# Batch 0's channel-128 transform ahead of the cosine transform, its row copied by ScalarE, the second weight chunk's products on GpSimd

## The chip, the cores and the metric

One NeuronCore of one Trainium2 chip runs the whole program. The metric is the device time of one execution in microseconds (us). One profiled execution per kernel gives a trace; the others are only timed. Engines are named as in the profile: PE is TensorE (PEld its weight loads), DVE is VectorE, ACT is ScalarE, POOL is GpSimd, and SPq is the queue of SyncE, which issues most DMAs.

## The reference, cut to what matters

```python
# x: (8, 3008, 256) float32; w_in: (256, 2048), w_out: (2048, 256), both float64
X = np.fft.fft(np.fft.fft(x, axis=1), axis=2).real     # FNet mixing
h = X.reshape(8 * 3008, 256) @ w_in
g = np.where(h > 0, h, np.exp(np.minimum(h, 0)) - 1)   # ELU
return g @ w_out
```

## The kernel before: the parts that the change touches

The kernel computes the sequence transform as matrix products with cosine and sine matrices (`MC`), using the symmetries of both axes: the input is folded to even and odd parts, and each batch has a cosine result `Rr` and a sine result `Ir` for channels 0 to 127. Channel 128 has no partner and is a single row. The channel transform is folded into the first weight matrix: `Wc` and `Ws` are made from `w_in` by small products ("folds"), chunk by chunk of 256 columns. The main loop then has 376 steps; each makes a cosine product `H <- Rr, Wc`, an even part `E` on VectorE, which adds channel 128 (`Rb` times a per-column factor `wex`), and a sine product `H <- Ir, Ws`, followed by ELU and the second layer. Row 127 of `Ir` carries the channel-128 row too.

The weights arrive as 64-bit floats and are turned into 32-bit ones by bit operations, in chunks. Each chunk has four parts; a "shared" one has its arithmetic on ScalarE and GpSimd:

```python
def fields(self):            # VectorE: exponent to a scratch t ("u", "v", ..., one buffer each), mantissa to dst
    ...
def power(self):             # ScalarE: exponent field; if shared also lo and dst to float
    act(self.t, self.t, func=AF.Relu, scale=8.0, bias=ebias)
    if self.shared: ...
def round(self):             # shared: GpSimd add; else VectorE
    ...
def scale(self):             # VectorE: sign into t; shared: GpSimd multiplies dst by t; else VectorE
    ...
```

Each fold's row for channel 128 must become a column. It goes through DRAM:

```python
def put_chunk(c):            # ScalarE copies the fold from PSUM to Ws and Wc
    ...
def spread_last_row(q):      # row 127 of Ws -> wx in DRAM -> two columns of wex
    queue.dma_start(out=wx_dr[:, c], in_=Ws[127:128, c])
    queue.dma_start(out=wex[:, 2*q : 2*q + 2], in_=wx_dr[:, c].rearrange("o (f p) -> p (o f)", p=128))
```

What is emitted when is a sorted list of events `at(t, fn)`, with `T` = 4.8 for a step. Negative times are the start; the hardware engines each run their own instructions in that order.

```python
for _ in range(62):                                     # filler matmuls on zeros
    mm(idle, zero, zero[:, 0:1].to_broadcast([128, 512]), True)
...
at(-13.0, lambda: dft_now(R_even, 1, "pA")); at(-12.9, lambda: dft_now(R_even, 0, "pB"))
at(-12.8, begin_x_even)                                 # channel 128, two transforms, after the cosine ones
...
at(-5.7, lambda: nc.sync.dma_start(out=Ir[127:128, 0:RUN], in_=Rb[127:128, 0:RUN]))
at_chunk(-5.0, w1_chunks[2])
```

## Time and profile before

| | before |
|---|---|
| executions known when the prediction was made | 1994.29, 1993.30, 1985.84; profiled one 1984.7 |
| span of the trace | 1982.9 |
| TensorE busy | 1960.3 (99%) |
| first sine product / second step's even part / ninth step's even part, start | 37.84 / 46.76 / 102.19 |

In the order of time, a line has its start, its length, engine, source line, operation, what it writes and reads, the shapes and the count of instructions merged into it. In brackets stands how long the engine was idle before it and what ended that. The granted clock is the share of full speed that TensorE's clock had; half clock is 0.50. A DMA lands when its semaphore reports its data. The prediction below shows and reads the lines of the kernel before.

The second step's even part (counting from one; the steps of the source count from zero) and the ninth's serve as marks in what follows: up to the first lie the parts that the change moves, and between the two the remaining weights are converted.

### The profile page before, as it was taken

The numbers are of one execution on the slowest core, as the hardware profiler recorded it, in microseconds if no ns is written. First come the engines' busy times: TensorE is split into PE (matmuls) and PEld (weight loads), VectorE is DVE, ScalarE is ACT, GpSimd is POOL, SyncE is SP. The second block draws the span as 40 slices with busy tenths as digits, with TensorE's granted clock in tenths as the row PEclk, the third lists the DMA queues.
The fourth block names the chain that finished last, engine by engine and source line by source line (L and its number), as shares of the span: only waits on it lengthen the run. The fifth ranks groups of instructions, "written<-read, shape, count | busy, mean of one in ns | idle before, by whom it ended". The sixth has DMA issues, their size and how long they took to land.

```text
span 1982.9 us, 26811 instructions
## 1 busy us (share of the span) xinstructions
PE 1960.3 (99%) x8896; PEld 1661.3 (84%) x8896; DVE 1280.8 (65%) x2342; ACT 861.0 (43%) x1651; POOL 1333.5 (67%) x1820
## 2 busy tenths in 40 slices
PE   8899999999999999999999999999999999999998
PEld 5788888888888888888888888888888888888887
DVE  7866656666666656676566666666556765666665
ACT  3544444443444444444444443444444444344443
POOL 2678757786577756777667775678657776455655
PEclk9999999999999999999999999999999999999999
DMA  8227200121011110011100211003010110100101
GB/s 322 86 20 64 46 16 16 38 59 21 16 19 45 45 29 12 18 43 46 28 11 20 61 28 27 11 19 86 9 21 12 20 22 14 16 12 12 22 10 23
DMA packets 256044, 71.61 MB, mean 36 GB/s; under 512 B 244303, under 2 KB 245092, under 8 KB 255394
## 3 DMA queue, kind: packets, MB, share of 16 engines
q1 hardware_dynamic: 251330, 57.05, 14.5%
q0 software_dynamic: 2400, 12.59, 1.9%
q8 instruction: 70, 1.15, 0.2%
q14 instruction: 68, 0.56, 0.1%
q10 hardware_dynamic: 2176, 0.26, 0.1%
HBM read 45.02 MB, written 24.80 MB: 35 GB/s over the span
## 4 chain that ended last, share of the span: by engine, by line
PE 94%; DVE 3%; DMA 1%; ACT 1%; issue 0%; POOL 0%; DVEq 0%; POOLq 0%; ACTq 0%; SPq 0%
PE H L353 38%; PE pB L353 16%; PE pD L353 16%; PE pC L353 16%; PE pA L353 8%; DVE E L715 0%; DMA Ir<-Rb 0%; DMA xl<-in_x_dram,ix 0%; DVE o L426 0%; DVE G L741 0%; DMA wex<-wx 0%; DVE e L426 0%; DMA wx<-Ws 0%; DVE v L359 0%; ACT w L365 0%
## 5 line engine op out<-in xcount | busy, mean ns | idle before, releaser
L362 POOL TENSOR_TENSOR G<-G 128x256 f32<-128x256 f32 x1472 | 1057.5, 728 | 580.4 <-DVE G L741 466.0
L715 DVE SCALAR_TENSOR_TENSOR E<-Rb,wex,H 128x256 f32<-128x256 f32 x752 | 328.0, 478 | 608.2 <-PE H L353 603.5
L365 ACT ACTIVATE G<-H 128x512 f32<-128x512 f32 x376 | 224.5, 597 | 950.2 <-DVE G L725 950.2
L353 PE MATMUL H<-Ir,Ws 128*128 128x256 f32 x1504 | 388.6, 381 | 11.3 <-DVE E L715 6.6
L353 PE MATMUL H<-Rr,Wc 128*128 128x256 f32 x1504 | 386.4, 379 | 0.0
L353 PE MATMUL pC<-G,WT 128*128 128x256 f32 x1472 | 377.8, 379 | 0.0
L353 PEld LDWEIGHTS H<-Rr,Wc 128*128 128x128 f32 x1504 | 285.1, 190 | 53.2 <-issue 2.5
L353 PEld LDWEIGHTS H<-Ir,Ws 128*128 128x128 f32 x1504 | 277.1, 189 | 62.5 <-DVE E L715 11.6
L353 PEld LDWEIGHTS pC<-G,WT 128*128 128x128 f32 x1472 | 279.7, 190 | 38.0
L725 DVE SCALAR_TENSOR_TENSOR G<-E,H 128x512 f32<-128x512 f32 x376 | 257.4, 685 | 40.5 <-PE H L353 2.7
L741 DVE SCALAR_TENSOR_TENSOR G<-G,H 128x512 f32<-128x512 f32 x376 | 256.0, 681 | 32.2 <-ACT G L365 32.1
L741 DVE SCALAR_TENSOR_TENSOR G<-M,G 128x512 f32<-128x512 f32 x376 | 257.1, 684 | 0.0
L353 PE MATMUL pA<-G,w 128*128 128x256 f32 x800 | 234.1, 379 | 0.5 <-issue 0.5
L353 PE MATMUL pB<-G,w 128*128 128x256 f32 x800 | 234.0, 379 | 0.0
L365 ACT ACTIVATE G<-G 128x512 f32<-128x512 f32 x376 | 233.3, 620 | 0.0
L365 ACT ACTIVATE M<-G 128x512 f32<-128x512 f32 x376 | 224.2, 596 | 0.0
L365 ACT ACTIVATE M<-M 128x512 f32<-128x512 f32 x376 | 221.0, 588 | 0.1
L353 PE MATMUL pD<-G,WT 128*128 128x256 f32 x736 | 219.1, 379 | 1.5 <-DVE v L359 1.5
L353 PE MATMUL pB<-G,WT 128*128 128x256 f32 x736 | 219.2, 379 | 0.5 <-POOL G L362 0.5
L353 PE MATMUL pD<-G,w 128*128 128x256 f32 x736 | 218.9, 379 | 0.0
L353 PEld LDWEIGHTS pA<-G,w 128*128 128x128 f32 x800 | 151.9, 190 | 21.5 <-POOL w L362 0.9
L353 PEld LDWEIGHTS pB<-G,w 128*128 128x128 f32 x800 | 152.0, 190 | 20.7
(136 smaller groups left out, 1332.8 us busy)
## 6 DMA issues: line engine op xcount, KB each, us to landing
out_dram<-ot SPq DMA_DIRECT2D x496, 32.0 KB
xl<-in_x_dram SPq DMA_DIRECT2D x16, 768.0 KB
MC<-dft_mats SPq DMA_DIRECT2D x4, 1131.0 KB
out_dram<-ot SPq DMA_DIRECT2D x256, 2.0 KB
Rb<-r SPq DMA_DIRECT2D x10, 376.0 KB
raw<-in_moe_w_in_dram SPq DMA_DIRECT2D x6, 512.0 KB
raw<-in_moe_w_out_dram SPq DMA_DIRECT2D x6, 512.0 KB
out_dram<-ot SPq DMA_DIRECT2D x64, 28.0 KB
```

Of the source, the lines that this page charges most:

```text
L353: nc.tensor.matmul(out_, lhsT=lhsT, rhs=rhs, start=start, stop=stop, skip_group_check=True)
L362: pin(nc.gpsimd.tensor_tensor(out=o, in0=a, in1=b, op=op))
L365: pin(nc.scalar.activation(out=o, in_=i, func=func, **kw))
L715: nc.vector.scalar_tensor_tensor(out=S.E[:, c], in0=Rb[:, cols(i)], scalar=wex[:, f : f + 1], in1=S.H[:, c], op0=ALU.mult, op1=ALU.add,)
L725: nc.vector.scalar_tensor_tensor(out=two(S.G[:, 0:512])[:, :, ::-1], in0=two(S.E), scalar=2.0, in1=two(S.H), op0=ALU.mult, op1=ALU.subtract,)
L741: nc.vector.scalar_tensor_tensor(out=o, in0=e, scalar=-1.0, in1=h, op0=ALU.add, op1=ALU.max)
```

## The change

It takes away the one DMA that TensorE waits for, brings channel 128 to the front so that its row is there early, drops 16 fillers, and gives chunk 1's products to GpSimd. Chunk 1's fold moves behind the first sine product, and chunk 2 is no longer converted ahead of the first even part but after it, beside chunk 3. The core of the diff (cut):

```diff
-            c in (2, 3),
+            c in (1, 2, 3),                       # chunks with shared arithmetic
...
-        e = spool.tile([128, GW], FP, tag="G", bufs=3, name="xb")       # 128 x 768, the value broadcast
...
+        e = spool.tile([128, 6], FP, tag="xe0", bufs=1, name="xe0")     # broadcast as TensorE reads it
...
-    for _ in range(62):
+    for _ in range(46):
...
+    at(-13.1, lambda: dft_now(state["x_even"], 1, "pC"))     # ahead of R_even's transforms
+    at(-13.1, lambda: dft_now(state["x_even"], 0, "pD"))
...
-    at(-5.7, lambda: nc.sync.dma_start(out=Ir[127:128, 0:RUN], in_=Rb[127:128, 0:RUN]))
-    at_chunk(-5.0, w1_chunks[2])
...
+    at(-10.88, lambda: act(Ir[96:128, 0:RUN], Rb[96:128, 0:RUN]))
...
+    at(0.95, w1_chunks[2].fields)                 # after the first even part, beside chunk 3
+    at(0.96, w1_chunks[2].power)
+    at(0.97, w1_chunks[2].round)
+    at(1.7, w1_chunks[2].scale)
...
-        t = (c - 2) * T + 4.7 if c > 1 else 1.0   # fold of chunk 1: behind the first sine product
+        t = (c - 2) * T + 4.7 if c > 1 else 2.3
```

More of the change, by code (lines that the diff above doesn't have):

```diff
@@ L480, in fold_first @@
         vtt(d, a, g, ALU.subtract)
-        e = spool.tile([128, GW], FP, tag="G", bufs=3, name="xb")
-        vtt(
-            e[:, 0:768].rearrange("p (m d) -> p m d", d=128),
-            a.unsqueeze(2).to_broadcast([128, 6, 128]),
-            g.unsqueeze(2).to_broadcast([128, 6, 128]),
-            ALU.add,
-        )
+        e = spool.tile([128, 6], FP, tag="xe0", bufs=1, name="xe0")
+        vtt(e, a, g, ALU.add)
         return e
@@ L497, in dft_mms @@
                 ps[:, 0:n],
-                stat[:, m * width : m * width + 128],
+                stat[:, m * width : m * width + 128]
+                if width > 1
+                else stat[:, m : m + 1].to_broadcast([128, 128]),
                 MC[ri, kodd][:, c : c + n],
@@ L528, in mms @@
         def mms(self, par, ps):
-            dft_mms(ps, self.ri, self.kodd, par, self.stat, 127 if self.ri else 128)
+            width = 1 if self.first else 127 if self.ri else 128
+            dft_mms(ps, self.ri, self.kodd, par, self.stat, width)
             if par:
@@ L1041, with begin_x_even @@
     at(-25.8, w1_chunks[0].round)
+    def begin_x_even():
+        state["x_even"] = Dft(0, 0, 0, fold_first(L_first), ring=Rb, first=True)
     at(-25.5, load_rest)
@@ L1044 @@
     at(-24.9, w1_chunks[0].scale)
-    at(-24.8, lambda: fold_now("c2 e2 E2 o3 o2 c0 e0 c1 e1 E0 EO0"))
+    at(-24.8, lambda: fold_now("c2 e2 E2 o3 o2"))
+    at(-24.5, begin_x_even)
+    at(-24.4, lambda: fold_now("c0 e0 c1 e1 E0 EO0"))
     at(-20.8, w2_chunks[2].load)
@@ L1052 @@
     at(-12.9, lambda: dft_now(R_even, 0, "pB"))
-    def begin_x_even():
-        xb = fold_first(L_first)
-        state["x_even"] = Dft(0, 0, 0, xb, ring=Rb, first=True)
-        dft_now(state["x_even"], 1, "pC")
-        dft_now(state["x_even"], 0, "pD")
-    at(-12.8, begin_x_even)
+    at(-13.1, lambda: dft_now(state["x_even"], 1, "pC"))
+    at(-13.1, lambda: dft_now(state["x_even"], 0, "pD"))
     at(-13.05, lambda: spread_last_row(0))
+    at(-11.5, lambda: state["x_even"].copy())
     at(-11.0, lambda: fold_now("O2 o0 o1 O0 EO2"))
-    at_chunk(-10.0, w1_chunks[1])
-    at(-8.5, R_even.copy)
-    at(-8.4, R_even.plus)
-    at(-8.3, R_even.minus)
-    at(-8.2, lambda: dft_now(I_even, 1, "pA"))
-    at(-8.1, lambda: dft_now(I_even, 0, "M"))
-    at(-6.0, lambda: state["x_even"].copy())
-    at(-5.9, lambda: state["x_even"].plus())
-    at(-5.8, lambda: state["x_even"].minus())
-    at(-5.7, lambda: nc.sync.dma_start(out=Ir[127:128, 0:RUN], in_=Rb[127:128, 0:RUN]))
-    at_chunk(-5.0, w1_chunks[2])
+    at(-10.9, lambda: state["x_even"].plus())
+    at(-10.89, lambda: state["x_even"].minus())
+    at(-10.88, lambda: act(Ir[96:128, 0:RUN], Rb[96:128, 0:RUN]))
+    at(-10.8, w1_chunks[1].fields)
+    at(-10.79, R_even.copy)
+    at(-10.78, w1_chunks[1].power)
+    at(-10.6, R_even.plus)
+    at(-10.59, R_even.minus)
+    at(-10.5, lambda: dft_now(I_even, 1, "pC"))
+    at(-10.5, lambda: dft_now(I_even, 0, "M"))
+    at(-10.4, w1_chunks[1].round)
+    at(-10.3, w1_chunks[1].scale)
+    at(0.95, w1_chunks[2].fields)
+    at(0.96, w1_chunks[2].power)
+    at(0.97, w1_chunks[2].round)
+    at(1.7, w1_chunks[2].scale)
     at(1.3, lambda: fold_now("EO1"))
@@ L1103 @@
     for c in range(1, 8):
-        t = (c - 2) * T + 4.7 if c > 1 else 1.0
+        t = (c - 2) * T + 4.7 if c > 1 else 2.3
         at(t, lambda c=c: fold_chunk(c))
-        t = (c - 1) * T + 1.4 if c > 1 else 2.0
+        t = (c - 1) * T + 1.4 if c > 1 else 3.0
         at(t, lambda c=c: put_chunk(c))
```

## The prediction

> **What bounds the kernel now.** I read the busy shares first, then the chain that ended last by engine, then the table of stretches to find where TensorE is idle, then TensorE's order of time and the other engines' around that place.
>
> Page of the kernel before, parts 1 and 4:
>
> ```profile
> PE 1960.3 (99%) x8896; PEld 1661.3 (84%) x8896; DVE 1280.8 (65%) x2342; ACT 861.0 (43%) x1651; POOL 1333.5 (67%) x1820
> ...
> PE 94%; DVE 3%; DMA 1%; ACT 1%; issue 0%; POOL 0%; DVEq 0%; POOLq 0%; ACTq 0%; SPq 0%
> ```
>
> TensorE is the bound. Only 1982.9 - 1960.3 = 22.6 us of the span are without a matmul, and no change that leaves the matmuls alone can win more. The stretches (us, busy time and count of each engine, granted clock, DMA share, GB/s) say where they lie:
>
> ```profile
> 0.00:20.00 20.00, 18.86 (x74) 8.91 (x75) 13.45 (x28) 3.38 (x7) 2.97 (x13) 1.00 0.93 362
> 20.00:30.00 10.00, 10.00 (x33) 6.01 (x32) 9.41 (x18) 2.63 (x5) 1.17 (x2) 1.00 1.05 392
> 30.00:34.00 4.00, 3.17 (x14) 2.27 (x12) 3.24 (x8) 1.33 (x4) 2.56 (x2) 1.00 0.99 406
> 34.00:38.00 4.00, 0.16 (x1) 0.19 (x2) 3.23 (x4) 3.50 (x7) 2.35 (x2) 0.91 1.00 389
> 38.00:41.00 3.00, 3.00 (x7) 2.19 (x8) 1.07 (x2) 0.79 (x3) 1.61 (x2) 0.56 1.06 377
> 41.00:48.00 7.00, 6.03 (x23) 4.09 (x22) 4.43 (x9) 1.82 (x4) 1.85 (x1) 1.00 0.21 69
> 48.00:100.00 52.00, 46.21 (x201) 37.13 (x200) 45.27 (x77) 28.58 (x57) 31.22 (x43) 1.00 0.25 82
> ```
>
> The diff touches the first 50 us only. There are 1.14 us idle at the start, 4.67 in 33 to 38, 0.97 before 48, and 5.8 in 48 to 100, where VectorE is 87% busy converting weights. DMA is full (share about 1) until about 42 us. TensorE in order of time at that place:
>
> ```profile
> 1.14 16.29 PE L353 MATMUL M<-zero 128*128 128x512 bf16 x62 [1.14 <-DVE zero L340]
> ...
> 37.84 2.04 PE L353 MATMUL H<-Ir,Ws 128*128 128x256 f32 x4 [4.67 <-DMA Ir<-Rb]
> 39.68 2.55 PE L353 MATMUL pA<-MC,e 128*128 128x376 f32 x6
> 42.07 2.06 PE L353 MATMUL pB<-MC,e 128*128 128x376 f32 x6
> 43.97 1.89 PE L353 MATMUL H<-w,CC 128*128 128x256 f32 x8
> 45.69 1.03 PE L353 MATMUL H<-Rr,Wc 128*128 128x256 f32 x4
> ```
>
> 62 filler matmuls on zeros end at 17.3. The first sine product then waits 4.67 us for a 3 KB row, Ir<-Rb, sent at 28.50 into a full DMA queue and landed at 37.71 (the trace's semaphore record): 9.2 us. At half clock its four matmuls take 2.04 instead of 1.03 and the next six 2.55 instead of 2.07, 1.5 us more. The even part of step 1 starts at 46.76 when TensorE has made its product.
>
> **What the Trainium skill says.** "TensorE: Matmul & The Clock Gate", Part 1 (What's actually happening): the clock falls to half after an idle window of about 3.4 us, on a free-running 3413 ns grid. The trace agrees: half clock for 3.413 us from 37.248, after idleness from 33.2. "DMA: Bandwidth & Descriptors", Queues, rings and completion order: each DMA engine consumes its ring in order; the row's 9.2 us behind matrices and weights agree. "SBUF — State Buffer", Who interferes with whom: GpSimd and a two-port VectorE operation exclude each other; one tensor_scalar of the conversion took 1.51 us beside GpSimd against 0.42 elsewhere, so it agrees. "ScalarE: Activation LUTs", What ACT_TABLE_LOAD costs: an ACTIVATE is 186 ns + 0.833 ns an element; the trace's 512-element ones take 0.60 to 0.66, so my estimate from that page for the new 752-element row copy is 0.81.
>
> **The change part by part.**
> - Fillers 62 to 46. Warm ones start 0.217 apart, so the first fold starts 16 x 0.217 = 3.5 earlier, at 13.8. The cosine matrix lands at 15.48, when this fold ends. Unpaid by itself: fillers are no work.
> - Channel 128 first, its stationary operand one column broadcast instead of a 128x768 tile: takes one VectorE add of 0.95 away for one of 0.16. The six transforms (about 1.9 each) run 15.6 to 27.0 instead of 19.0 to 30.4. VectorE's last odd fold ends at 23.85 - 0.8 = 23.1, just when TensorE wants it. I assume a broadcast weight load costs the same 0.19.
> - The row DMA becomes a ScalarE copy on 32 partitions, 0.81, after the Rb sum and before the Ir sums overwrite rows 96 to 126. The DMA wait goes. Rr is then complete at about 26.4, Ir at 28.6.
> - First step: its wex column comes 11.4 us after ScalarE's put of chunk 0 (19.86 to 31.28 in the trace); that put now ends at 16.4, so wex is there at 27.8. Even part 28.6 to 29.4, sine product 29.5 to 30.4, against 37.84: **8 us earlier here**.
> - Chunk 1's two products go to GpSimd (1.29 and 1.27). VectorE loses two instructions of 0.69, ScalarE gains two (0.66 and 0.61). Chunk 1 is ready at 29.9, its fold runs 30.4 to 32.1 (now behind the sine product).
>
> **What takes the gain back.** The next matmuls are R_odd on the odd cosine matrix, which landed at 34.72 in the trace. That DMA is issued at 20.33 in a queue that runs full, with nothing changed in front of it. So TensorE idles about 32.1 to 34.8 and R_odd starts about 4.9 earlier than 39.68, not 8. The idle time is below 3.4, so I expect no half clock.
>
> A second brake lies in step 1, whose even part needs wex for chunk 1: put by ScalarE, row out to DRAM, column back in. Before:
>
> ```profile
> 37.80 0.36 ACT L365 ACTIVATE Ws<-H 128x256 f32<-128x256 f32 x1
> ...
> 38.19 0.31 SPq L392 DMA_DIRECT2D wx<-Ws  x1
> ...
> 41.50 0.37 SPq L394 DMA_DIRECT2D wex<-wx  x1
> ```
>
> The column landed at 44.43, a slack of 2.3 to 46.76. In the new order two weight chunks (2 and 3) are converted together after the first even part, and the next one (second matrix, chunk 0) needs the scratch u that chunk 2's second GpSimd product still reads. Worked out: fields of chunk 2 at 29.4 to 30.1, ScalarE's three operations for it 29.9 to 31.8, for chunk 3 31.8 to 33.6; GpSimd's products 31.8 to 33.1, 33.7 to 35.0, 35.0 to 36.3, 36.3 to 37.5. So the fields of the next chunk are free at 36.3, and through the port lock end at about 38.2 (before: 37.23). ScalarE's three operations end at 39.8, and Ws is put at 40.1, **two us later than before**. The DMA backlog still ends near 42.4. Row and column took 6.2 together in the backlog, about 3.4 without; I take 4.5, so wex lands at about 44.6.
>
> Meanwhile R_odd ends at 38.6, the fold at 40.3, step 1's cosine product at 41.3: they wait for wex. Step 1's even part starts at 44.6 instead of 46.76. From there all engines keep the old order (I compared it engine by engine: it is the same), so the rest shifts by **2.1 us**. Sum: 8 gained at the first step, 3 lost to the matrix, 3 more to the scratch and the wex round trip.
>
> **Rivals.**
> 1. The full gain: 4.67 idle + 1.5 half clock + the earlier start, 5 to 8 us. For it: the wait is real and on the chain. Against: the landing at 34.72. It would give about 1986.
> 2. Only the matrix binds: 4.9 us, 1988.4. For it: wex for chunk 1 could come sooner if the conversion overlaps better than I worked out. Against: the scratch u exists once.
> 3. Nothing or a small loss: the wex trip behind the backlog takes 6.2 again (46.3), TensorE's idle 41 to 45 fills a window and costs half clock, so 0 to +1.5. For it: VectorE bound in 48 to 100 us. Against: the backlog ends soon after the row is sent.
> 4. Spread between executions: three runs from 1985.84 to 1994.29 and a profiled one at 1984.7, larger than any of these.
>
> **Range and chances.** 1993.3 - 2.1 = 1991.2 from the median; the mean of the four executions is 1989.5, less 2.1 is 1987.4. As I can't tell which group the new runs fall into, I say 1990. The range, 1983 to 1995.5, covers the four executions (1984.7 to 1994.3) shifted by -2 to +1. Two per cent is 40 us, more than the 22.6 us of all idle TensorE time; slower by 40 us would need damage in the steady state, whose order is unchanged. So within 2% is nearly sure: 0.98, 0.01 to each side.
>
> **What the profile after will show.** No Ir<-Rb DMA and no wait on it; first sine product near 29.5 (my sum of the front is wrong if it is beyond 31); TensorE's largest early wait before pA<-MC,e, on the MC DMA, near 34.8, then one before the second H<-Ir,Ws near 45, released by VectorE's E after the wex DMA. Ws put for chunk 1 near 40, not 38. 46 fillers, VectorE some 2 us less busy, GpSimd some 2.6 more. Wrong would be: R_odd well before 34; the put before 38 (then the gain is 4 to 5); a slower broadcast weight load; or idle TensorE time after 100 us that was not there.

## The result

Six executions of the changed kernel took 1984.04 to 1986.31, median 1984.97; six of the kernel before have the median 1986.23. The ratio is 0.9982 with a 95% interval from 0.9963 to 1.0001, which takes in 1. Such a ratio is the mean time of one kernel's fast runs over that of the other's of the same rounds, so not quite the ratio of the medians. "Fast" there means not over 1.5% above the fastest; executions that are 4 to 12 us longer than the rest (0.2% to 0.6%) pass as fast. There are such executions, and they matter here. I call those over 1990 us long and the others quick; the cut is mine. The quick ones before: 1985.84, 1986.42, 1986.04, 1985.47, mean 1985.94. The changed kernel's six, all quick: mean 1985.05. So the change is worth 0.9 us in that comparison, where the prediction had about 2 from its working and 3.3 (1993.3 less 1990) from its base.

The page of the changed kernel, parts 1 and 4, shows TensorE as busy as before; its 2.3 us less are 4.2 less of fillers (12.09 against 16.29) and some half clock more. Sixteen fillers of 0.217 would be 3.5; the other 0.7 is luck, as nine fillers instead of twelve ran at about half speed at the start (0.427 apart):

```profile
PE 1958.0 (99%) x8880; PEld 1661.6 (84%) x8880; DVE 1281.2 (65%) x2340; ACT 862.8 (44%) x1654; POOL 1336.2 (67%) x1822
...
PE 94%; DVE 2%; DMA 2%; ACT 1%; issue 0%; POOL 0%; DVEq 0%; POOLq 0%; ACTq 0%; SPq 0%
```

The stretches of the changed kernel (us; busy time and count of PE, PEld, DVE, ACT, POOL; granted clock; DMA share; GB/s):

```profile
34.00:38.00 4.00, 4.00 (x15) 2.50 (x14) 1.58 (x2) 0.19 (x1) 4.00 (x4) 1.00 1.01 388
38.00:41.00 3.00, 1.32 (x7) 0.81 (x5) 3.00 (x5) 2.21 (x5) 0.80 (x2) 1.00 0.96 346
41.00:48.00 7.00, 3.08 (x9) 2.27 (x10) 6.10 (x11) 3.82 (x8) 2.63 (x2) 0.62 0.27 83
48.00:100.00 52.00, 47.08 (x199) 38.69 (x198) 44.01 (x74) 26.93 (x55) 30.92 (x43) 0.95 0.25 82
```

The hole of 34 to 38 us is gone. A new one has come at 38 to 48: TensorE is busy 4.4 of 10 us there. The granted clock falls to 0.62 in 41 to 48 and is 0.95 over the next 52 us, where it had been 1.00. TensorE in order of time:

```profile
29.98 1.10 PE L353 MATMUL H<-Ir,Ws 128*128 128x256 f32 x4 [1.45 <-DVE E L713]
30.92 1.89 PE L353 MATMUL H<-w,CC 128*128 128x256 f32 x8
33.56 2.13 PE L353 MATMUL pA<-MC,e 128*128 128x376 f32 x6 [0.75 <-DMA MC<-dft_mats]
...
41.18 1.13 PE L353 MATMUL H<-Rr,Wc 128*128 128x256 f32 x4 [1.86 <-ACT Wc L365]
46.05 2.07 PE L353 MATMUL H<-Ir,Ws 128*128 128x256 f32 x4 [3.74 <-DVE E L713]
47.92 2.82 PE L353 MATMUL pA<-MC,o 128*128 128x376 f32 x6
```

The first sine product starts at 29.98 instead of 37.84, 7.9 us earlier. The second one starts at 46.05 instead of 47.68, only 1.6 earlier: TensorE waited 1.86 for ScalarE's put of chunk 1 and 3.74 for the even part, and took 2.07 and 2.82 at half clock where 1.13 and 2.06 are full-clock lengths. The even part was held by its column:

```profile
40.50 0.36 ACT L365 ACTIVATE Ws<-H 128x256 f32<-128x256 f32 x1
...
40.88 0.31 SPq L392 DMA_DIRECT2D wx<-Ws  x1
...
42.07 0.36 SPq L394 DMA_DIRECT2D wex<-wx  x1
...
45.13 0.87 DVE L713 SCALAR_TENSOR_TENSOR E<-Rb,wex,H 128x256 f32<-128x256 f32 x2 [0.86 <-DMA wex<-wx]
```

Why the put came at 40.50 and not near 38 is in GpSimd's and VectorE's order of time:

```profile
35.98 2.49 POOL L362 TENSOR_TENSOR w<-w,pow 128x512 f32<-128x512 f32 x2
...
37.28 1.48 DVE L214 TENSOR_SCALAR pow<-w 128x512 int32<-128x512 int32 x1 [2.42 <-DMA raw<-in_moe_w_in_dram]
```

VectorE could not start the next chunk's fields before GpSimd's product for chunk 2, the first of the two that begin at 35.98, had read the scratch u. (The profile names a DMA as the releaser; that DMA was long in, and the start at 37.28 is the end of one product of about 1.25.) It then took 1.48 beside the second product, against 0.41 for the next one.

How the start of the even part moved against the kernel before, step by step, in the profiled executions (counted from one):

| even part of step | 1 | 2 | 3 | 4 | 5 | 6 | 7 | 9 | 100th |
|---|---|---|---|---|---|---|---|---|---|
| before, us | 31.97 | 46.76 | 56.65 | 65.75 | 75.23 | 83.46 | 89.89 | 102.19 | |
| changed, difference | -3.00 | -1.63 | -1.39 | -1.37 | -0.55 | -0.66 | -0.22 | -0.21 | -0.25 |

So 1.6 us are won at the second even part, and 1.4 of them are gone by the seventh. What is left at the ninth stays to the start of the last step. After that it goes too: TensorE waits 0.33 for GpSimd before some of its last products (at 1973.08), and the two traces end at 1982.9 (before) and 1983.1 (changed).

How far such marks can be trusted shows in b_late, an experiment below: up to 100 us it is the kernel before, yet its second even part lies at +0.47 and its ninth at +0.70. And the trace of the kernel before is one of its quickest executions (1984.7, where its quick means are 1985.9 to 1986.7), so differences against it understate a gain. Differences below about 0.7 between single traces decide nothing by themselves.

Three terms make up that 1.4. The interval from the second to the third even part is 10.13 instead of 9.89: half clock from 42.6 to 49.4. The one from the fourth to the fifth is 10.29 instead of 9.48: the column of the fifth step took 7.2 us from its put to its landing, instead of 6.4, beside the loads of batch 1. Its even part, before and then changed:

```profile
75.23 0.87 DVE L715 SCALAR_TENSOR_TENSOR E<-Rb,wex,H 128x256 f32<-128x256 f32 x2 [0.32 <-DMA wex<-wx]
```

```profile
74.67 0.87 DVE L713 SCALAR_TENSOR_TENSOR E<-Rb,wex,H 128x256 f32<-128x256 f32 x2 [1.13 <-DMA wex<-wx]
```

The interval from the sixth to the seventh is 6.88 instead of 6.43: TensorE, which had waited 3.01 in the fifth step, ran at half clock from 76.75 to 80.16 and was still behind. The lines of that place, before and then changed:

```profile
76.15 1.13 PE L353 MATMUL H<-Ir,Ws 128*128 128x256 f32 x4 [2.20 <-DVE E L715]
77.12 1.89 PE L353 MATMUL pB<-G,w 128*128 128x256 f32 x8
```

```profile
75.60 1.13 PE L353 MATMUL H<-Ir,Ws 128*128 128x256 f32 x4 [3.01 <-DVE E L713]
76.57 3.43 PE L353 MATMUL pB<-G,w 128*128 128x256 f32 x8
```

The same eight products take 3.43 instead of 1.89.

### The profile page after: what moved, and what is told of

It reads as the page before. It is cut to its first block, busy times and chain, and to the rows that moved or that the text cites. A ratio compares the mean times of both kernels' runs of the same rounds, so it can differ in the third digit from the quotient of the medians.

```text
span 1983.1 us, 26783 instructions
## 1 busy us (share of the span) xinstructions
PE 1958.0 (99%) x8880; PEld 1661.6 (84%) x8880; DVE 1281.2 (65%) x2340; ACT 862.8 (44%) x1654; POOL 1336.2 (67%) x1822
## 3 DMA queue, kind: packets, MB, share of 16 engines
HBM read 45.02 MB, written 24.80 MB: 35 GB/s over the span
## 4 chain that ended last, share of the span: by engine, by line
PE 94%; DVE 2%; DMA 2%; ACT 1%; issue 0%; POOL 0%; DVEq 0%; POOLq 0%; ACTq 0%; SPq 0%
PE H L353 38%; PE pB L353 16%; PE pD L353 16%; PE pC L353 16%; PE pA L353 8%; DMA raw<-in_moe_w_in_dram 1%; DMA xl<-in_x_dram,ix 1%; DVE E L713 0%; DMA wex<-wx 0%; DVE G L739 0%; POOL G L362 0%; DMA wx<-Ws 0%; DVE o L426 0%; DVE e L426 0%; DVE v L359 0%
```

## The experiments

Theory A: the head start is lost in two places, first to the wait for the second step's column and then to half clock and longer column trips. Its rivals are named at each run. Each kernel was run in five rounds beside the kernel before, in four groups of kernels that each ran on one chip. "Quick mean" has the long executions left out; "ninth" is the start of the ninth even part against the first trace of the kernel before (102.19), in the one profiled execution.

| kernel | executions, of them long | quick mean | before in that group: quick mean | second even part | ninth |
|---|---|---|---|---|---|
| a_again | 5, 2 | 1985.93 | 1986.39 | 44.83 | -0.03 |
| b_row_act | 6, 2 | 1982.87 | 1986.39 | 44.18 | -1.22 |
| a_row_dma | 6, 2 | 1987.88 | 1986.39 | 48.67 | +3.35 |
| a_fill62 | 6, 1 | 1986.49 | 1986.39 | 45.96 | +0.37 |
| a_c2early | 6, 2 | 1984.91 | 1986.45 | 44.82 | -0.37 |
| a_vec1 | 6, 1 | 1985.66 | 1986.45 | 44.92 | -0.28 |
| a_col | 6, 2 | 1984.89 | 1986.45 | 44.70 | -0.03 |
| b_row_late | 6, 0 | 1983.94 | 1986.45 | 44.23 | -1.83 |
| b_late | 5, 0 | 1987.15 | 1986.47 | 47.22 | +0.70 |
| a_warm | 5, 0 | 1985.26 | 1986.47 | 44.84 | -0.95 |
| a_c2_col_late | 5, 0 | 1984.95 | 1986.47 | 44.53 | +0.65 |
| b_row_col_late | 5, 0 | 1985.53 | 1986.47 | 44.28 | -0.33 |
| a_late | 6, 0 | 1986.01 | 1986.69 | 45.00 | -0.36 |
| b_row_late2 | 6, 0 | 1983.87 | 1986.69 | 44.19 | -1.36 |
| b_row_warm_late | 6, 0 | 1985.28 | 1986.69 | 45.25 | +0.59 |

All outputs were correct. The 95% interval lies clear of 1 for a_row_dma (1.0008 to 1.0042), b_row_late, b_row_late2 and b_row_warm_late (0.9955 to 0.9994) alone. The quick means have no interval and rest on my cut.

### a_again: the changed kernel once more

No edit.

> The changed kernel unaltered, for its time against the kernel before on one chip and in the same rounds. Theory A (the head start of 8 us at the first sine product shrinks to 1.6 at the second step's even part, because that waits for the wex column, and is then eaten by half-clock stretches and longer column trips before 100 us): 0.2 to 1 us faster than before, ratio 0.9995 or so. Rival B (the first three runs of before, 1993.3 as median, were its true time and the change is worth 2 to 3 us): 2 to 3.5 us faster, ratio 0.9985.

The quick executions are 0.5 us below the kernel before; the ratio is 1.0004 (0.9991 to 1.0017), with the two long ones in it. Theory A's size fits, and rival B falls: over the first comparison (0.9), this one and a_late (0.7, with later transforms that cost something themselves) the change is worth 0.5 to 0.9 us. The spread of quick executions, 3 to 4 us, can barely carry such a size. Its profiled execution happened to be a long one of 1992.76, and its head is like that of the first trace (second even part 44.83, ninth -0.03). The excess arises at one place, TensorE at 194 us:

```profile
194.50 4.18 PE L353 MATMUL H<-MC,xe 128*8 128x377 f32 x24 [4.96 <-POOL xe L362]
```

In the first, quick trace of the changed kernel the same line reads

```profile
189.29 2.09 PE L353 MATMUL H<-MC,xe 128*8 128x377 f32 x24
```

These are the channel-128 transforms of batches 1 to 7. Their data are gathered element by element from about 130 us on; GpSimd folds them when the last of it has landed. The waits of the long execution between 185 and 200 us (who waited for whom: us, times, longest):

```profile
POOL xs L362 <- DMA xs<-xe_dr: 5.9, 1, 5.9
...
PE H L353 <- POOL xe L362: 5.0, 1, 5.0
```

After the wait of 5.0 the clock is halved for 6.8 us. The thirty-first step is 7.7 us late, and it stays so to the end.

### b_row_act: the kernel before with the row copy alone

```diff
-    at(-5.7, lambda: nc.sync.dma_start(out=Ir[127:128, 0:RUN], in_=Rb[127:128, 0:RUN]))
+    at(-5.7, lambda: act(Ir[96:128, 0:RUN], Rb[96:128, 0:RUN]))
```

> The kernel before with one part alone: the channel-128 row goes to Ir by a ScalarE copy instead of the DMA; order, fillers and VectorE's conversion of chunk 1 stay. Theory A: the 4.67 us wait becomes one for the odd cosine matrix (landing 33.4 to 34.8), first sine product near 33, R_odd near 35; put of chunk 1 stays at about 38 to 38.5 as its scratch is free early, so the second step's even part starts at 44 to 45 (46.76 before, 45.13 in the whole change): at least as good as the whole change there, 0.3 to 2 us faster in all. Rival C (the early order, channel 128 first and chunk 1 on GpSimd, is what wins): second even part near 46.5, no gain.

TensorE in order of time:

```profile
33.69 1.10 PE L353 MATMUL H<-Ir,Ws 128*128 128x256 f32 x4 [1.12 <-DVE E L715]
35.66 2.13 PE L353 MATMUL pA<-MC,e 128*128 128x376 f32 x6 [0.87 <-ACT raw L365]
...
45.10 2.08 PE L353 MATMUL H<-Ir,Ws 128*128 128x256 f32 x4 [2.81 <-DVE E L715]
```

The first sine product is 3.7 us later than in the whole change, and the second is 0.95 earlier. The put of chunk 1 stays at 38.51, so the column landed at 44.07 instead of 45.02. Rival C falls: the early order wins nothing that lasts. Four of six executions took 1982.80 to 1982.92, 3.5 below the kernel before; two were long, and the profiled one (1995.34) shows 9.3 us of wait at the same channel-128 transforms. The ratio, 0.9994, has those two in it.

### a_row_dma: the change with the row sent by DMA again

```diff
-    at(-10.88, lambda: act(Ir[96:128, 0:RUN], Rb[96:128, 0:RUN]))
+    at(-10.88, lambda: nc.sync.dma_start(out=Ir[127:128, 0:RUN], in_=Rb[127:128, 0:RUN]))
```

> The changed kernel with the row sent by DMA again, all else changed. The row is issued near 24.4 behind both odd matrices and lands near 36. Theory A: first sine product near 36 instead of 29.98, R_odd near 39, but the second even part still waits for wex at about 45 (45.13 to 45.8), and the total is within 0.7 us of the changed kernel. Rival D (the row's DMA was the wait that cost the time): second even part 3 to 5 us later, total 3 us or more slower.

```profile
37.54 2.04 PE L353 MATMUL H<-Ir,Ws 128*128 128x256 f32 x4 [8.94 <-DMA Ir<-Rb]
39.37 2.88 PE L353 MATMUL H<-w,CC 128*128 128x256 f32 x8
```

My expectation missed: the second even part came at 48.67, as rival D has it, not at 45. The wait of 8.94 brought half clock from 31 to 41 us, the fold of chunk 1 now lies behind the sine product, and with both TensorE itself is late. The total is 2.0 above a_again's quick mean, more than theory A's 0.7 and less than rival D's 3. So the row copy is a true gain under either order. What remained open was whether the rest of the change adds to it.

### a_fill62: the change with 62 fillers

```diff
-    for _ in range(46):
+    for _ in range(62):
```

> The changed kernel with 62 fillers again. They end 3.5 us later (17.3); six transforms follow 2.8 us later than in the changed kernel. Theory A: first even part near 31.5 instead of 28.97, and as ScalarE's and GpSimd's conversions of chunks 2 and 3 start from it, the put of chunk 1 moves from 40.5 to about 42.5 and the second even part from 45.13 to about 47; total 0.5 to 2 us slower than the changed kernel. Rival E (the wex trip ends when the DMA backlog ends, whatever the put): second even part stays near 45, total the same.

First even part 30.27, put 41.28, second even part 45.96: each later, each by less than I had said (31.5, 42.5, 47). The total, 0.6 above a_again's quick mean, is at the low end of theory A's 0.5 to 2. The column lands less late than it is issued, which is half of rival E. Over the traces of both kernels and four variants, the row left at 38.19, 38.90, 39.73, 40.88, 41.68 and 42.70, and its column landed at 44.43, 44.07, 44.72, 45.02, 45.85 and 45.85: 4.5 us of issue time move the landing by 1.8 at most. The bulk of matrices and weights is in at about 42.7, and in none of these traces is the column there before 44.

### a_c2early: chunk 2 converted early again

```diff
-    at(0.95, w1_chunks[2].fields)
-    at(0.96, w1_chunks[2].power)
-    at(0.97, w1_chunks[2].round)
-    at(1.7, w1_chunks[2].scale)
+    at(-10.2, w1_chunks[2].fields)
+    at(-1.7, w1_chunks[2].power)
+    at(-1.6, w1_chunks[2].round)
+    at(0.95, w1_chunks[2].scale)
```

> The changed kernel with one thing undone: chunk 2 of the first matrix is converted ahead of the first even part again, no longer in a pair with chunk 3, so its GpSimd products are done before chunk 3's and the scratch u comes free earlier. Theory A1 (scratch u and the paired conversions delay the put of chunk 1, hence the wex column, hence the second even part): put of Ws chunk 1 near 36 to 38 instead of 40.5, column issued then, second even part 43.3 to 44.5 instead of 45.1; total 0.7 to 2 us faster than the changed kernel. Rival A2 (the column lands when the DMA backlog has drained, whatever the put): put earlier, but the second even part at 44.8 to 45.2 and no gain.

The put came at 39.34, 1.2 earlier, but the second even part at 44.82, no earlier than in a_again (44.83): A2 rather than A1. The scratch u does delay the put, but the put is not all that the column waits for. The quick mean is 1.0 below a_again's, in another group and within the spread.

### a_vec1: chunk 1's products on VectorE

```diff
-            c in (1, 2, 3),
+            c in (2, 3),
```

> The changed kernel with chunk 1's two products on VectorE again. Theory A: VectorE has 1.4 us more before the Ir sums, first even part at 29.3 to 29.8 instead of 28.97, put of chunk 1 within 0.7 of 40.5, second even part 45.0 to 45.8, total within 0.7 us of the changed kernel: the products' engine hardly matters. Rival F (GpSimd's two extra products push chunk 2's and 3's products and so the put): put near 39, second even part near 44, about 1 us faster.

First even part 29.41, put 40.43, second even part 44.92, ninth -0.28: theory A. The move of chunk 1's products to GpSimd, the part that the change's name ends with, has no effect that these runs can see. Rival F falls.

### a_col: columns by TensorE instead of the trip through DRAM

```diff
...                                        # e127, a column with one 1, is made by GpSimd and ScalarE
+    def column(c):                          # row 127 of Ws as a column: Ws^T times a unit vector
+        for j in range(2):
+            f = 2 * c + j
+            mm(folds[c][:, j : j + 1], Ws[:, f * 128 : (f + 1) * 128], e127, j == 0)
+    def put_column(c):
+        act(wex[:, 2 * c : 2 * c + 2], folds[c][:, 0:2])
...
-        at(t + 0.01, lambda c=c: spread_last_row(c))
+        t = (c - 1) * T + (3.3 if c > 1 else 4.79)
+        at(t, lambda c=c: column(c))
+        at(t + 0.001, lambda c=c: put_column(c))
```

> The changed kernel with the wex columns of chunks 1 to 7 made by TensorE (row 127 of Ws times a unit column, two small products into the fold's own bank) and copied by ScalarE, in place of the row's trip to DRAM and back; chunk 0 keeps its trip. Theory A (the trip is the wait that binds the second even part and later ones): second even part at 42.5 to 43.5 instead of 45.1, step interval 3 to 4 (10.3 us in the changed kernel) back to about 9, and 1.5 to 4 us faster in all. Rival B (VectorE's conversions bind from 45 to 100 us whatever the column): second even part earlier, but the ninth step's within 0.5 us of the changed kernel's, total the same.

TensorE at the second step:

```profile
41.04 0.61 PE L356 MATMUL H<-e,Ws 128*128 128x1 f32 x4 [1.26 <-ACT Wc L368]
42.51 2.07 PE L356 MATMUL H<-Rr,Wc 128*128 128x256 f32 x4 [0.86 <-ACT wex L368]
```

The column was there at 42.45, but the even part started at 44.70: the cosine product itself now came late and at half clock, and VectorE was busy with the next chunk to 44.1. So there was little to win here: in the changed kernel, too, VectorE is busy to 44.26, 0.76 before the column lands (45.02). And the edit puts the cosine product behind the column's products, where it ends at 44.58. The interval from the fourth to the fifth even part went back to 9.10, as theory A said. But the ninth even part is where it was (-0.03): with the extra products in its order TensorE has no idle time left from 79 to 96 us, and the interval from the sixth to the seventh even part is 7.35, against 6.88 in the changed kernel. That is rival B's outcome, though by TensorE's time and not by VectorE's.

### b_row_late and b_late: the later transforms of channel 128

```diff
-    at(25 * T + 1.35, fold_ext)
-    at(25 * T + 4.75, dft_ext)
+    at(27 * T + 1.35, fold_ext)
+    at(27 * T + 4.75, dft_ext)
...                                        # their five followers also two steps later
-                s0 + (28, 34, 38, 42)[n], 2, b,
+                s0 + (28, 34, 38, 42)[n] + 2 * (b == 1), 2, b,
-            step = s0 + (28, 38)[kodd]
+            step = s0 + (28, 38)[kodd] + 2 * (b == 1)
```

b_row_late has b_row_act's edit as well; b_late is the kernel before with this edit alone.

> The kernel before with the row copied by ScalarE, and the channel-128 transforms of batches 1 to 7 two steps (9.5 us) later, with batch 1's own transforms and its row spread two steps later too. Theory G (the executions that are 8 to 11 us slower are those in which the gather of channel 128 lands after TensorE wants it at about 190 us: two traces show 5.0 and 9.3 us of wait there and then 7 to 10 us of half clock, and two traces of quick executions none): no execution more than 3 us above its fastest, all at about 1983. Rival H (those executions come from elsewhere): one in four of them still near 1993.

> The kernel before with one thing changed, far from the studied change: the channel-128 transforms of batches 1 to 7 two steps later, with batch 1's own transforms and row spread. Theory G (slow executions of the kernel before, such as two of the three that made its median 1993.3, come from TensorE waiting there for the gather): all executions within 3 us of 1986, no wait over 1 us before the channel-128 transforms. Rival H: one in five still at 1992 to 1998.

Neither had a long execution; b_late's longest is 3.1 us above its fastest, just over the 3 that I had said. Of the executions with the transforms in their old place 24 of 101 were long (12 of 49 of the kernel before, 12 of 52 of the others). Of those with the later place 0 of 39 were, the longest 1989.34. Three long executions were profiled (1992.76, 1995.34 and 1990.47); all three show TensorE waiting before these transforms, 5.0, 9.3 and 3.8 us, and then half clock, and no quick trace shows such a wait. Theory G holds. What makes the gather's last part land later in some executions was not found. The later place itself costs something: the ninth even part of b_late lies at +0.70 and the sixty-first at +1.25, so about 0.5 us, and in b_row_late 0.8. In the long execution of a_again the gather was behind over its whole length and did not just stall at its end: from the first to the last of its four write-outs (`xe_dr<-x`) it took 38.3 us (150.10 to 188.44), against 30.6 (147.74 to 178.31) in the quick trace of the same kernel.

### a_warm: fillers in the waits

```diff
+    def fill(i, n):                         # adds zeros to the open bank
+        for _ in range(n):
+            mm(steps[i].H, zero, zero[:, 0:1].to_broadcast([128, 512]), False, False)
+    at(T + 0.1, lambda: fill(1, 12))
+    at(4 * T + 2.1, lambda: fill(4, 8))
```

> The changed kernel with zero matmuls added into the open bank where TensorE waits for the column: twelve ahead of the second even part, eight ahead of the fifth. They add zeros, so results stay right. Theory W (the half clock after those waits is what eats the head start from 1.6 us at the second even part to 0.2 at the seventh): no half clock in 40 to 82 us, the six sine transforms that took 2.8 to 3.1 at 2.06, the ninth even part 0.5 to 1 us earlier than in the changed kernel, total 0.5 to 1 us faster. Rival T (the lengthened column trips alone eat it): half clock gone but the ninth even part within 0.2 us, total the same.

```profile
41.86 2.77 PE L353 MATMUL H<-zero 128*128 128x512 bf16 x12
45.76 1.13 PE L353 MATMUL H<-Ir,Ws 128*128 128x256 f32 x4 [1.12 <-DVE E L713]
46.73 2.06 PE L353 MATMUL pA<-MC,o 128*128 128x376 f32 x6
```

From the same second even part as a_again's (44.84), with no half clock before 1977 us, the ninth is at -0.95, against -0.03 to -0.36 in three traces of the changed kernel (a_late's among them): theory W, 0.6 to 0.9 us. This is one trace, but the place fits: the interval from the second to the third even part is 9.89, as in the kernel before, against 10.13, 10.41 and 10.53 in the three. The eight fillers of the fifth step were misplaced: they stand behind its even part in the order, so they ran after the wait and held the sine product up by 1.7. They did keep half clock away there, but that only made up for it: the fifth interval is 0.5 longer than in the changed kernel (8.63 for 8.13), the sixth 0.45 shorter (6.43 for 6.88). The gain is from the first twelve. The quick mean, 1.2 below the kernel before, fits but does not prove it.

### a_c2_col_late and b_row_col_late: combinations

The edits above, added together; no new ones.

> The changed kernel with three mends together: chunk 2 converted early (scratch u free sooner), columns made by TensorE, channel-128 transforms two steps later. Theory A plus G: the second even part no longer waits for column or conversions, 42 to 43.5 against 45.1; no slow executions; 1 to 3 us faster than the changed kernel's quick runs, 1982 to 1984. Rival B (the work of TensorE and VectorE to 100 us absorbs it): second even part earlier but the ninth within 0.5 us of the changed kernel's, 1985.

> The kernel before with the row copied by ScalarE, columns made by TensorE and channel-128 transforms two steps later: the candidate to beat both. Theory A plus G: second even part 42.3 to 43.5, no slow executions, 1981 to 1983.5. If the column's extra products of TensorE (0.8 us each, seven of them) cost more than the trip: slower than the same kernel without the column, whose quick runs were 1983.3 to 1985.4.

Both miss the hoped-for second even part (44.53 and 44.28, not 42 to 43.5), and neither beats b_row_late. In the first the total is rival B's (1984.95 for 1985), but not by its reading: the ninth lies at +0.65, and the changed kernel's at -0.03 to -0.36, further apart than B's 0.5. In the second the columns by TensorE cost more than the trip they save: its mean is 1.6 above b_row_late's of another group.

### a_late, b_row_late2, b_row_warm_late: side by side, without long executions

a_late is the changed kernel with the later transforms. b_row_late2 is b_row_late again. b_row_warm_late is that with fillers (ten and eight).

> The changed kernel with the channel-128 transforms two steps later, so that it has no slow executions. Theory A: its executions lie within 3 us of each other, 0 to 1.5 us below the kernel before's quick ones, and 1 to 2 us above those of the row copy alone with the same mend, run beside it. Rival J (the whole change and the row copy alone are worth the same, the difference in earlier runs was chance): means within 0.5 us of each other.

> The row copy alone with the later channel-128 transforms, a second time: all executions between 1983 and 1986, none slow, mean 2 to 3 us below the kernel before's quick ones (theories A and G). Rival J: mean at 1985 to 1986 this time.

> The same with zero matmuls in the two waits for the column (ten ahead of the second even part, eight ahead of the fifth). Theory W (half clock after the waits costs what it did in the changed kernel): no half clock from 40 to 82 us, ninth even part 0.3 to 0.8 us earlier than without them, mean 0.3 to 1 us lower, 1982.5 to 1983.5: the best of all. If the fillers hold the even part up: 0 to 0.5 us slower.

This is the clean comparison, on one chip: the whole change 1984.80 to 1987.52, the row copy alone 1983.19 to 1984.63, means 2.1 apart. The two traces show 0.9 of that at the last step; for the rest there are only the times. Rival J falls: the rest of the change costs back about three quarters of what its one part wins. The fillers did not help the row copy: 1985.28, or 1.4 slower, and I had said 0.3 to 1 faster or at most 0.5 slower. This time the first set was itself in the way. Its ten products end at 45.21 in the bank that the even part reads, and the even part starts then, released by TensorE and not by the column, where b_row_late2's starts at 44.19:

```profile
45.25 0.87 DVE L715 SCALAR_TENSOR_TENSOR E<-Rb,wex,H 128x256 f32<-128x256 f32 x2 [0.77 <-PE H L353]
```

Part of that is not theirs: the first even part, ahead of them, was 0.8 late already. Again the second set stood behind the even part, and in that trace half clock came at 76 us all the same. So this run does not tell what well placed fillers would do.

b_row_late is the version to keep of those that ran: twelve executions of it have the mean 1983.9 and the maximum 1985.36, with ratios of 0.9974 (0.9950 to 0.9998) and 0.9968 (0.9949 to 0.9987), in which the kernel before has three and six long executions of eleven. This stands against a quick mean of 1985.1 to 1986.0 for the whole change, and against 49 executions of the kernel before with a mean of 1988.4, the long ones included.

## Why the prediction was right or wrong

- **The base was wrong.** "1993.3 - 2.1 = 1991.2 from the median": two of the three executions were over 1993, and the mean that I then took mixed the two kinds. I called it spread ("I can't tell which group the new runs fall into") without asking the trace what could make two groups. The stated 1990.0 is therefore 5 us above the measured 1984.97. That the range held it says little, as it is 12.5 us wide for a change of about 1. The runs show a second kind of execution in 24 of 101, from a wait at 190 us which the profile of the quick execution cannot show; there it only shows transforms that follow closely on their data. That the two executions over 1993 were of this kind is inferred, as they have no trace.
- **The first sine product was right**: 29.98 against 29.5. R_odd: the matrix did hold it, as said, but landed at 33.43 instead of 34.72, so 33.56 against 34.8.
- **The second brake was right in mechanism and nearly in size**: put 40.50 (40.1 predicted), column at 45.02 (44.6), even part at 45.13 (44.6), gain 1.63 in place of 2.1; a_again 1.93. The weight I gave to the scratch was too high: a_c2early put 1.2 earlier and won nothing there, as the column is held by the transfers in front as well.
- **The step that failed is "From there all engines keep the old order ..., so the rest shifts by 2.1 us".** The same order does not keep the same lengths. The 1.63 became 0.21 by the ninth step: 0.24 by half clock, 0.81 by the longer trip of the fifth step's column, 0.45 by half clock again, and 0.08 given back in between. I had worked out that TensorE would wait from 41.3 for an even part that starts at 44.6. With the 0.9 from there to the sine product, as I had it in the first step, that is an idle time of about 4.2 us, and I did not draw the clock from it, though I had done so for the earlier wait. Rival 3 names it. a_warm puts the two half-clock terms together at 0.6 to 0.9. The longer trip is shown as a term by the interval of 9.10 that a_col has without it; why it is longer is open.
- **The sum "8 gained, 3 lost, 3 more lost"** should read 7.9 gained at the first sine product, 6.2 lost by the second, 1.4 more by the ninth.
- **Smaller points.** The first fold started at 13.07 and not at 13.8, by the three slow fillers fewer, and gained nothing by it, as the cosine matrix held the next product to 15.62. TensorE's largest early wait was to be the one for the odd matrix, 2.7 us; it was 0.75, and the largest were 3.74 and 1.86 in the second step. "No change that leaves the matmuls alone can win more" than 22.6 us is not so: half-clock time counts as busy, as the prediction's own 1.5 us show. The row copy took 0.83, against the estimate of 0.81; 512-element ACTIVATEs that read a bias column took up to 0.72, not 0.66. GpSimd is 2.7 busier, as said. VectorE is not 2 us less busy (1281.2 against 1280.8): its operations became longer beside GpSimd's, such as 1.48 in place of 0.41. The broadcast weight load costs nothing visible: the six matmuls on xe take 2.14 (first after a wait) and 2.07, against 2.06 for those on xb. Within 2% was sure, and was so.
- **Still open**: why the fifth step's column takes 0.8 longer when it starts a microsecond earlier; and why the quick executions of one kernel differ by up to nearly 4 us. Half clock that comes on a free-running grid is a candidate, and one pair of traces supports it. With the same first 100 us, the kernel before was at half clock from 37.25 to 40.66 and b_late from 35.13 to 41.96, and the second is 0.70 later at the ninth even part. The timed executions have no trace; of the kernel before beside the experiments, the 16 quick ones with a mean granted clock of 0.997 took 1986.65 on average and the 15 with 0.998 took 1986.15, but the two groups overlap widely.

## What to carry to other kernels

When a wait is removed near the start, follow each later step's waits to the point where the order repeats, with their clock, and not just to the first step that is earlier. Test the one part that takes the wait away by itself: here it was worth 2.8 us, the whole change 0.7. And when the few executions of a kernel fall into two groups, look for a place where data land just when they are wanted; moving that consumer two steps later took away every long execution.

## What the Trainium skill lacked or had wrong

- "TensorE: Matmul & The Clock Gate", Part 1 (What's actually happening) halves the clock after an idle window of about 3.4 us. In these runs a window need not be idle throughout. In a_vec1 a gap of 2.15 us (28.27 to 30.42) inside one window of 3.41 (28.2 to 31.6, TensorE busy 1.25 of it) brought half clock for the next 3.4. In the changed kernel 2.26 idle in the window 73.3 to 76.75 did. In the kernel before a gap of 2.20 that lay across a window's border (74.79) did not. I laid the grid of each trace over its first 105 us (from 20 us on), leaving out the three kernels whose one-column products also count as busy. At full clock, every window in which TensorE was busy for at most 1.33 us (the longest: b_row_warm_late, 72.70 to 76.11) was followed by half clock, and none in which it was busy for 1.61 or more (the shortest: before, 64.55 to 67.96).
- No page that I read has how much a round trip of a 1 KB row through DRAM into columns of 4-byte elements grows beside other transfers: about 4.1 us from the row's issue to the column's landing in the changed kernel as the bulk transfers ended (40.88 to 45.02), 6.2 in the kernel before amid them (38.19 to 44.43), and 6.9 in the changed kernel's fifth step, beside the loads of batch 1 (67.71 to 74.57).
- "DMA: Bandwidth & Descriptors" says nothing of how much the end of a long element-wise gather varies: the wait for it was none in the quick executions and 3.8 to 9.3 us in three others, of kernels that differ only in their first 50 us.
- "SBUF — State Buffer", Who interferes with whom, agrees: 1.48 us beside a GpSimd product against 0.41.
